# Nine attention blocks ahead of the MLP, x through DRAM, and the weight decode on VectorE

## The chip, the core and the metric

One core of a Trainium2 chip runs the whole program in one launch. TensorE (PE) multiplies, VectorE (DVE) and ScalarE (ACT) do the elementwise work, GpSimd (POOL) some of it and the scattered stores, and SyncE (SP) issues most transfers. The metric is the device time of one execution in microseconds, the median of three runs.

## The reference

```python
def _attn_ref(u, v, z):
    scores = scale * np.matmul(z, z.transpose(0, 2, 1))   # 8 x 3072 x 3072, d_qk 64
    attn = np.maximum(scores, 0.0) ** 2
    out = np.matmul(attn, v)                              # d_model 256
    return (u * out).astype(np.float32)

def _moe_ref(x, w_in, w_out):                             # 24576 tokens, 256 -> 2048 -> 256
    h = x @ w_in
    g = h * (1.0 / (1.0 + np.exp(-h)))
    return (g @ w_out).astype(np.float32)

def _moe2_ref(x, w_gate, w_output_gate, w1, w2):          # 8 experts, 256 -> 1024 -> 256
    e_idx = np.argmax(x @ w_gate, axis=1)
...
        h = np.maximum(x[mask] @ w1[e], 0.0)
        out[mask] = gate_w[mask, None] * eom[mask, e, None] * (h @ w2[e])
```

The output of the first feeds the second, and that of the second the third. The scores are symmetric, since the same z stands on both sides.

## The kernel before

The attention's work is 48 blocks of 512 queries (n = 6 b + q, six for each of eight batches b), and a block has 24 steps, one for each tile of 128 keys. Every factor is kept as a high and a low part in float32r, and each product is three matmuls (high by high, low by high, high by low).

- A **direct step** has 2 matmuls of 512 columns for the scores (L269, L270), Relu and Square on ACT (L272, L273), the high part on ACT (L275) or DVE (L277), the low part on DVE (L251), and 6 matmuls of 512 columns into the accumulator `acc` (L293 to L295).
- A **mirrored step** takes the scores of an earlier block of the same batch instead of computing them. The earlier block stored them in the DRAM tile `sym` (L239). SP loads them with four transfers for each step (L225), DVE transposes (L232) and makes the low part, ACT the high part, and 6 matmuls follow. A block q has 4 q mirrored steps, from block 3 on. The loads go through `raw`, which has four buffers, together with the loads of z and V.
- An **MLP step** is one sixteenth of the MLP of a block's 512 tokens: 6 matmuls of 512 columns (L324), a sigmoid on ACT (L326), a product on DVE (L328), the high part on ACT (L331), the low part on DVE (L333), and 12 matmuls of 256 columns into `acc` (L358 to L360). After the last step ACT copies `acc` into the record `rec` with two copies (L350). PSUM has two buffers for `acc`: where attention and MLP alternate, each has one.

After its MLP a block is routed: 32 dot products of `rec` with the gate's weights on DVE (L368, the program calls them dots), some small operations that pick the expert, a count on PE (L375), and four scattered stores on POOL (L434) into the DRAM tile `scr`. When 46 blocks are routed, a snapshot of the counts (L456 to L483) sets up the first 39 tiles of 512 tokens of the third part, which SP loads from `scr` (L572). 22 smaller tiles come behind. This third part is the same in both kernels.

The sixteen 512-column pieces of the MLP's weights are decoded on chip (`w_decode`, `w_parts`): each is loaded into a `rec` buffer (L825), and takes seven operations on DVE (L840 to L843, L854 to L856), one on ACT and two on POOL (L857, L858). Of batch 0 POOL also makes the low parts of V (L94).

One list of steps sets the order on all engines. A step's front part is issued at its place, the middle one place later and its products three places later (`LOOK`). Other work (loads, decode, dots, stores) is a list of tasks, each with a due place, a release place and a cost. A step gives a budget, which pays for tasks that are released but not yet due, in the order of their due places, and the search stops after 60 entries that are not released:

```python
                if rel <= i and budget <= 0:
                    break
                k += 1
                if k > 60:
                    break
```

Before, blocks 0 and 1 and the first seven steps of block 2 run alone, then the MLP of block 0 alone, then that of block 1 step by step with block 2. From block 3 on two MLP steps stand ahead of every three attention steps. The loads of u and the product with the attention's output (`finish`, L303) go into the buffer `xf`, and the split of x (L204, L206) follows at once, so x never leaves the chip.

## Time and profile before

| | |
|---|---|
| median of three runs | 5292.82 us (5292.71 to 5293.24) |
| profiled execution, its own time | 5293.77 us |
| its span in the profile | 5292.0 us |
| PE busy | 5189.7 us, 98% |
| DVE, ACT, POOL busy | 3897.6, 3234.9, 491.2 us |

A PE matmul's record is longer than its share of the engine, since they are pipelined: PE's pace is read from one start to the next. What PE loses is the length of a stretch less the matmuls in it at that pace.

### The profile page before, as it was taken

How to read it: one execution, taken by the hardware profiler on the slowest of the kernel's cores; microseconds unless marked ns; L12 is line 12 of the kernel's file. 1: busy time of each engine (PE TensorE's matmuls, PEld its weight loads, DVE VectorE, ACT ScalarE, POOL GpSimd, SP SyncE). 2: the span in 40 equal slices, each digit the busy share in tenths (PEclk: the TensorE clock that was granted, in tenths of full speed). 3: DMA queues.
4: the chain of work that ended last, by engine and by line, in shares of the span. 5: the costliest groups of instructions: out<-in, count | busy, mean ns of one | idle time of the engine just before them, and what ended most of it. 6: DMA issues, size and time to landing. Idle time of an engine off the chain costs nothing.

```text
span 5292.0 us, 88328 instructions
## 1 busy us (share of the span) xinstructions
PE 5189.7 (98%) x30026; PEld 4529.6 (86%) x30026; DVE 3897.6 (74%) x9627; ACT 3234.9 (61%) x5804; POOL 491.2 (9%) x503
## 2 busy tenths in 40 slices
PE   7999999999999999999999999999999899999998
PEld 5888888888888888888888888888888799999998
DVE  8778767866786778677767877687677786666687
ACT  6655665666566666665666566656654455555576
POOL 3100000000000000000000000000000121111111
PEclk9999999999999999999999999999999899999999
DMA  5134324433442334234333432343333456555564
GB/s 155 57 81 86 102 80 92 93 89 77 86 104 85 81 77 110 81 77 84 108 80 82 87 106 75 83 91 95 86 83 80 133 171 201 175 175 175 178 229 157
DMA packets 1334523, 574.63 MB, mean 109 GB/s; under 512 B 1173421, under 2 KB 1206830, under 8 KB 1318192
## 3 DMA queue, kind: packets, MB, share of 16 engines
q1 hardware_dynamic: 1315248, 517.00, 38.1%
q0 software_dynamic: 18816, 51.93, 2.7%
q8 instruction: 237, 3.88, 0.3%
q14 instruction: 222, 1.82, 0.1%
HBM read 393.54 MB, written 178.42 MB: 108 GB/s over the span
## 4 chain that ended last, share of the span: by engine, by line
PE 84%; DVE 8%; ACT 3%; issue 2%; DMA 2%; SPq 0%; POOL 0%; DVEq 0%; ACTq 0%; POOLq 0%
PE ps L324 17%; PE ps L663 10%; PE acc L360 9%; PE acc L358 9%; PE acc L359 9%; PE acc L295 8%; PE acc L294 8%; PE acc L293 8%; PE ps L269 3%; PE ps L270 3%; DVE lo L251 1%; DMA raw<-sym 1%; DVE lo L333 1%; DVE junk L368 1%; DVE t L328 1%
## 5 line engine op out<-in xcount | busy, mean ns | idle before, releaser
L328 DVE TENSOR_TENSOR t<-ps,t 128x512 f32<-128x512 f32 x768 | 529.4, 689 | 655.5 <-ACT t L326 649.8
L359 PE MATMUL acc<-woutl,hi 128*128 128x256 f32 x3600 | 998.3, 277 | 0.0
L331 ACT ACTIVATE hi<-t 128x512 fp32r<-128x512 f32 x768 | 486.0, 633 | 764.1 <-DVE t L328 764.1
L294 PE MATMUL acc<-lo,vh 128*128 128x512 f32 x2304 | 911.1, 395 | 37.7 <-DVE lo L251 37.5
L295 PE MATMUL acc<-hi,vl 128*128 128x512 f32 x2304 | 910.9, 395 | 0.0
L293 PE MATMUL acc<-hi,vh 128*128 128x512 f32 x2304 | 903.3, 392 | 0.0
L360 PE MATMUL acc<-wouth,lo 128*128 128x256 f32 x3072 | 858.5, 279 | 42.5 <-DVE lo L333 42.4
L251 DVE TENSOR_TENSOR lo<-t,hi 128x512 fp32r<-128x512 f32 x1152 | 791.4, 688 | 130.9 <-ACT hi L275 128.9
L358 PE MATMUL acc<-wouth,hi 128*128 128x256 f32 x3072 | 853.9, 278 | 0.0
L359 PEld LDWEIGHTS acc<-woutl,hi 128*128 128x128 f32 x3600 | 678.0, 188 | 32.4
L368 DVE CUSTOM_DVE_ANT_0 junk<-rec,wg 128x256 f32<-128x256 f32 x1536 | 648.7, 422 | 35.3
L360 PEld LDWEIGHTS acc<-wouth,lo 128*128 128x128 f32 x3072 | 577.9, 188 | 53.0 <-DVE lo L333 50.9
L326 ACT ACTIVATE t<-ps 128x512 f32<-128x512 f32 x768 | 454.6, 592 | 265.5 <-PE ps L324 263.7
L358 PEld LDWEIGHTS acc<-wouth,hi 128*128 128x128 f32 x3072 | 577.6, 188 | 26.2
L294 PEld LDWEIGHTS acc<-lo,vh 128*128 128x128 f32 x2304 | 433.9, 188 | 158.3 <-DVE lo L251 56.5
L434 POOL DMA_INDIRECT scr<-rec,si x192 | 206.7, 1077 | 3767.2 <-DVE lo L251 1705.9
L264 ACT ACTIVATE hi<-t 128x512 fp32r<-128x512 f32 x468 | 295.8, 632 | 418.7 <-DVE t L232 333.9
L333 DVE TENSOR_TENSOR lo<-t,hi 128x512 fp32r<-128x512 f32 x768 | 523.6, 682 | 13.1 <-issue 0.2
L293 PEld LDWEIGHTS acc<-hi,vh 128*128 128x128 f32 x2304 | 434.2, 188 | 98.8
L295 PEld LDWEIGHTS acc<-hi,vl 128*128 128x128 f32 x2304 | 434.3, 189 | 91.4
L666 ACT ACTIVATE hi<-ps 128x512 fp32r<-128x512 f32 (+1 forms) x488 | 254.7, 522 | 396.9 <-PE ps L663 375.3
L668 DVE SCALAR_TENSOR_TENSOR lo<-ps,hi 128x512 fp32r<-128x512 f32 (+1 forms) x488 | 288.2, 591 | 245.8 <-ACT hi L666 244.0
(449 smaller groups left out, 10572.9 us busy)
## 6 DMA issues: line engine op xcount, KB each, us to landing
raw<-in_w_dram SPq DMA_DIRECT2D x122, 1024.0 KB
sym<-t SPq DMA_DIRECT2D x468, 256.0 KB
raw<-sym SPq DMA_DIRECT2D x1872, 64.0 KB
raw<-in_zT_dram SPq DMA_DIRECT2D x192, 128.0 KB
raw<-in_vp_dram SPq DMA_DIRECT2D x96, 256.0 KB
xf<-in_uT_dram SPq DMA_DIRECT2D x96, 256.0 KB
xg<-scr SPq DMA_DIRECT2D x39, 544.0 KB
x<-scr SPq DMA_DIRECT2D x304, 64.0 KB
```

The lines of the kernel that those rows point to most:

```text
L251: nc.vector.tensor_tensor(out=lo, in0=a, in1=r32(hi), op=ALU.subtract)
L293: nc.tensor.matmul(acc[:, c, :], h, hi, start=i == 0, stop=False)
L294: nc.tensor.matmul(acc[:, c, :], h, lo, start=False, stop=False)
L295: nc.tensor.matmul(acc[:, c, :], l, hi, start=False, stop=i == KT - 1)
L324: nc.tensor.matmul(ps, win_at(w, c, f_), x[c], start=c == 0 and i == 0, stop=c == ND - 1 and i == 2)
L328: nc.vector.tensor_tensor(out=g, in0=ps, in1=sg, op=ALU.mult)
L333: return lambda: nc.vector.tensor_tensor(out=lo, in0=g, in1=r32(hi), op=ALU.subtract)
L358: nc.tensor.matmul(y[:, s, :], a, wh, start=first and s % per_bank == 0, stop=False, skip_group_check=True)
L359: nc.tensor.matmul(y[:, s, :], a, wl, start=False, stop=False, skip_group_check=True)
L360: nc.tensor.matmul(y[:, s, :], l, wh, start=False, stop=last, skip_group_check=True)
L368: nc.vector.tensor_tensor_reduce(out=j, in0=a, in1=w, scale=1.0, scalar=0.0, op0=ALU.mult, op1=ALU.add, accum_out=res)
L663: nc.tensor.matmul(ps[:, 0:T], w[:, o:o + P], y[c][:, 0:T], start=c == 0 and j == 0, stop=c == ND - 1 and j == 2)
```

## The change

Blocks 0 to 8 run their attention alone, ahead of any MLP step. Their x therefore has to wait, and goes to DRAM: `finish` stores each half (two transfers for each block), and `load_x` brings it back through `raw` shortly before the MLP block, where `f_x` splits it. From block 9 on, an attention block takes 24, 22, 20, 18, 16 or 14 MLP steps by its place q in the batch, in eight groups, each ahead of three attention steps. An MLP block of 16 steps no longer ends where an attention block does.

The mirrored steps begin at block 4 of batch 0, so block 3's twelve become direct. POOL's part of the decode goes to DVE (`w_low`), and so do the low parts of V of batch 0. The decode tasks are released from place 24. The dots of block 45 become due ten places ahead of the last MLP block, where they were due at the end of the one before it.

```diff
@@ the constants
-EARLY = 0.95
+EARLY = 0.75
+LEAD = 9
+MIX = (24, 22, 20, 18, 16, 14)
...
-PRE = 7
@@ x of a block, kept in DRAM until its MLP block
         def load_u(b, q):
             t = mk(cp, [P, ND, TQ], F32, "xf", 1)
...
+        def load_x(n, c):
+            def f(t):
+                nc.sync.dma_start(out=t, in_=xd[n][:, c, :])
+            return f
+
+        def f_x(n, c):
+            def f(t):
+                if c == 0:
...
+                h, l = xs[n]
+                nc.scalar.activation(h[c], t, AF.Copy)
+                nc.vector.tensor_tensor(out=l[c], in0=t, in1=r32(h[c]), op=ALU.subtract)
+            return f
...
         def mirrored(b, q, k):
-            return k // NS < q and (b, q) >= (0, 3)
+            return k // NS < q and (b, q) >= (0, 4)
@@ att_items
-            early = (b, q) < (0, 2)
+            early = b * NQ + q < LEAD
...
-                    if (early and q and k % 2) or (not early and (q or k % 3)):
+                    if k % 2 and b + q or not early and (q or k % 3):
                         nc.scalar.activation(hi, a, AF.Copy)
                     else:
                         nc.vector.tensor_copy(hi, a)
...
                     if i == KT - 1:
                         later(1, 1.2, finish, 0)
-                        later(3, 1.2, lambda: split_x(b, q, hold == "last"), 0)
...
             def finish():
-                for c, x in enumerate(xs[(b, q)]):
+                n = b * NQ + q
+                xd[n] = dram.tile([P, ND, TQ], F32, name=f"x_{n}")
+                for c in range(ND):
+                    x = st["x"][:, c, :]
                     nc.vector.scalar_tensor_tensor(out=x, in0=st["acc"][:, c, :], scalar=AS, in1=x, op0=ALU.mult, op1=ALU.mult)
+                    nc.sync.dma_start(out=xd[n][:, c, :], in_=x)
@@ the order of the steps
-        order = [("a", 0, 0, KT), ("a", 1, 0, KT), ("a", 2, 0, PRE), ("m", 0, 0, NF1)]
-        for k in range(NF1):
-            order += [("a", 2, PRE + k, PRE + k + 1), ("m", 1, k, k + 1)]
...
-        for n in range(3, NBLK):
+        order = [("a", n, 0, KT) for n in range(LEAD)]
+        GA, todo = KT // 8, 0
+        for n in range(LEAD, NBLK):
             for g in range(8):
-                if n > 3 or g >= 2:
-                    j = (g - 2) % 8 * GM
-                    owed.append(("m", n - 1 if g >= 2 else n - 2, j, j + GM))
...
+                for _ in range(MIX[n % NQ] * (g + 1) // 8 - MIX[n % NQ] * g // 8):
+                    m = todo // NF1
+                    if (m + 1, 4) <= (n, g):
+                        order += [("m", m, todo % NF1, todo % NF1 + 1)]
+                        todo += 1
                 order += [("a", n, g * GA, (g + 1) * GA)]
...
+        for todo in range(todo, NBLK * NF1):
+            order += [("m", todo // NF1, todo % NF1, todo % NF1 + 1)]
@@ V, the loads of x, the decode and the route
-            return lambda t: split(t, hi, lo, due, None if b else nc.gpsimd)
+        def f_split(hi, lo, due):
+            return lambda t: split(t, hi, lo, due)
...
+            for c in range(ND):
+                prep(moe_at[n] - 3 + c, moe_at[n] - 3 + c if n == NBLK - 1 else moe_end[n - 2] if n > 1 else moe_at[0] - 4, load_x(n, c), f_x(n, c), att_step(n, KT - 1) + LOOK + 4)
...
-                nc.gpsimd.tensor_tensor(out=m, in0=t_bits, in1=r32(hi), op=ALU.subtract)
-                nc.gpsimd.tensor_tensor(out=lo, in0=m, in1=t_rem, op=ALU.add)
...
+        def w_low(k):
...
+                nc.vector.tensor_tensor(out=m, in0=t_val[k % 2], in1=r32(hi), op=ALU.subtract)
+                nc.vector.tensor_tensor(out=lo, in0=m, in1=t_rem, op=ALU.add)
                 w_load(k + 2)
...
-            task(job[0], 6, 1.9, w_decode(k))
-            task(job[0], 6, 1.3, w_parts(k))
+            task(job[0], KT, 2.4, w_decode(k))
+            task(job[0], KT, 1.6, w_parts(k))
+            task(job[0], KT, 1.4, w_low(k))
...
+            if n == NBLK - 3:
+                due = moe_at[NBLK - 1] - 10
             route_tasks(n, due, rel)
```

Three places show the order.

On PE, at the end of an MLP block in the middle of the kernel before (`acc_18534` is the MLP's accumulator, `acc_19339` the attention's, `ps` the scores or the MLP's first product):

```order
L358 MATMUL acc_18534<-wouth_99,hi_19357 128x256
L359 MATMUL acc_18534<-woutl_101,hi_19357 128x256
L360 MATMUL acc_18534<-wouth_99,lo_19358 128x256
L324 MATMUL ps_19434<-xo_19317,winh_94 128x512
L324 MATMUL ps_19434<-xo_19317,winl_96 128x512
L324 MATMUL ps_19434<-x_19318,winh_94 128x512
L324 MATMUL ps_19434<-xo_19317,winh_94 128x512
L324 MATMUL ps_19434<-xo_19317,winl_96 128x512
L324 MATMUL ps_19434<-x_19318,winh_94 128x512
L293 MATMUL acc_19339<-hi_19367,vh_115 128x512
```

The next MLP block's own products begin 24 matmuls further on. In the change, at the first such end (`acc_4314` and `acc_5157` are two MLP blocks' accumulators):

```order
L367 MATMUL acc_4314<-wouth_99,hi_5066 128x256
L368 MATMUL acc_4314<-woutl_101,hi_5066 128x256
L369 MATMUL acc_4314<-wouth_99,lo_5067 128x256
L275 MATMUL ps_5148<-hh_4015,hl_107 128x512
L276 MATMUL ps_5148<-ll_4016,hl_107 128x512
L367 MATMUL acc_5157<-wouth_98,hi_5089 128x256
L368 MATMUL acc_5157<-woutl_100,hi_5089 128x256
L369 MATMUL acc_5157<-wouth_98,lo_5090 128x256
```

Two matmuls of a direct step stand between an MLP block's last product and the next MLP block's first, and the attention's products come behind. On ACT the copies of that accumulator stand between two direct steps:

```order
L279 ACTIVATE t_1162_5125<-t_1162_5125 128x512
L281 ACTIVATE hi_5120<-t_1162_5125 128x512
L359 ACTIVATE rec_5142<-acc_4314 128x2x256 x2
L278 ACTIVATE t_1167_5151<-ps_5148 128x512
L279 ACTIVATE t_1167_5151<-t_1167_5151 128x512
```

There are 22 such ends in the change, and none before: 14 with a direct front between, as here, and 8 with nothing, where the front is that of a mirrored step.

On SP, in block 5 before (`sym_2_5` holds scores for mirrored steps, `zT` is z):

```order
L162 DMA raw_4810<-in_zT_dram 64x512
L163 DMA raw_4810<-in_zT_dram 64x512
L225 DMA raw_4881<-sym_2_5_2529 32x16x32 x4
L225 DMA raw_4898<-sym_2_5_2529 32x16x32 x4
L225 DMA raw_4925<-sym_2_5_2529 32x16x32 x4
L225 DMA raw_4948<-sym_2_5_2529 32x16x32 x4
L225 DMA raw_5001<-sym_3_5_3398 32x16x32 x4
L225 DMA raw_5018<-sym_3_5_3398 32x16x32 x4
L225 DMA raw_5045<-sym_3_5_3398 32x16x32 x4
```

and in the change, where between these loads no MLP step runs and a weight piece is loaded (`rec`, L833):

```order
L163 DMA raw_2476<-in_zT_dram 64x512
L164 DMA raw_2476<-in_zT_dram 64x512
L231 DMA raw_2495<-sym_2_5_1410 32x16x32 x4
L231 DMA raw_2512<-sym_2_5_1410 32x16x32 x4
L833 DMA rec_2529<-in_win_dram 128x1024
L231 DMA raw_2533<-sym_2_5_1410 32x16x32 x4
L231 DMA raw_2551<-sym_2_5_1410 32x16x32 x4
L231 DMA raw_2558<-sym_3_5_1822 32x16x32 x4
L231 DMA raw_2579<-sym_3_5_1822 32x16x32 x4
```

The weights' loads stood at rows 13 to 78 of SP before, and 14 of the 16 now stand among the tiles of blocks 4 to 9.

On DVE, the dots of block 45 before, ahead of the snapshot (L328 and L333 belong to MLP steps, `L` are the results):

```order
L333 TENSOR_TENSOR lo_46448<-t_10847_46445,hi_46447 128x512
L368 ISA junk_46486,L_45918<-rec_45831,wg 128x256
L368 ISA L_45918 128x1
L368 ISA junk_46488,L_45918<-rec_45831,wg 128x256
L368 ISA L_45918 128x1
L328 TENSOR_TENSOR t_10859_46499<-ps_46490,t_10858_46497 128x512
L333 TENSOR_TENSOR lo_46471<-t_10852_46468,hi_46470 128x512
L368 ISA junk_46517,L_45918<-rec_45831,wg 128x256
L368 ISA L_45918 128x1
L368 ISA junk_46519,L_45918<-rec_45831,wg 128x256
L368 ISA L_45918 128x1
L368 ISA junk_46521,L_45918<-rec_45831,wg 128x256
```

and in the change (L337 and L342 are the MLP's; the lines left out are more of L377):

```order
L337 TENSOR_TENSOR t_10884_46531<-ps_46522,t_10883_46529 128x512
L342 TENSOR_TENSOR lo_46484<-t_10874_46481,hi_46483 128x512
L337 TENSOR_TENSOR t_10889_46558<-ps_46549,t_10888_46556 128x512
L342 TENSOR_TENSOR lo_46534<-t_10884_46531,hi_46533 128x512
L377 ISA junk_46577,L_46576<-rec_46468,wg 128x256
L377 ISA L_46576 128x1
L377 ISA junk_46579,L_46576<-rec_46468,wg 128x256
L377 ISA L_46576 128x1
...
L377 ISA junk_46639,L_46576<-rec_46468,wg 128x256
L377 ISA L_46576 128x1
L410 TENSOR_REDUCE m_46641<-L_46576 128x4
```

All 32 dots of the block now follow on one another, before the pick (L410), whose result PE's count needs (`L384 MATMUL ps_46658<-ohc,ones 128x8`), and this count stands ahead of the next MLP front on PE.

## Rows read from the trace of the kernel before

**Rows 1.** The page's part 1, busy time by engine.

```profile
PE 5189.7 (98%) x30026; PEld 4529.6 (86%) x30026; DVE 3897.6 (74%) x9627; ACT 3234.9 (61%) x5804; POOL 491.2 (9%) x503
```

**Rows 2.** Windows by attention block (0, 1, 2, 6): length, busy, counts, clock.

```profile
core 0: us, PE busy (x) PEld busy (x) DVE busy (x) ACT busy (x) POOL busy (x), PEclk, DMA share, GB/s
6.80:74.20 67.40, 52.87 (x198) 38.34 (x199) 59.04 (x86) 46.92 (x82) 28.78 (x21) 0.97 0.56 174
74.20:137.90 63.70, 50.58 (x193) 37.25 (x192) 61.31 (x91) 46.81 (x80) 22.42 (x16) 0.95 0.46 132
137.90:277.10 139.20, 135.64 (x772) 117.22 (x771) 100.34 (x208) 88.34 (x152) 20.30 (x17) 1.00 0.18 58
520.50:612.80 92.30, 90.27 (x487) 76.47 (x486) 66.58 (x177) 65.56 (x114) 9.27 (x10) 1.00 0.35 112
```

**Rows 3.** Timeline of PE: start, duration, line, tile; 512 columns, then 256.

```profile
400.11 0.40 PE L295 MATMUL acc<-hi,vl 128*128 128x512 f32 x1
400.34 0.40 PE L324 MATMUL ps<-xo,winh 128*128 128x512 f32 x1
...
4090.29 0.28 PE L359 MATMUL acc<-woutl,hi 128*128 128x256 f32 x1
4090.41 0.28 PE L360 MATMUL acc<-wouth,lo 128*128 128x256 f32 x1
```

**Rows 4.** Waits of PE in the first 150 us: total, times, longest.

```profile
PE acc L294 <- DVE lo L251: 28.8, 25, 2.5
```

**Rows 5.** Timeline of DVE and of POOL in block 0.

```profile
55.07 1.77 DVE L251 TENSOR_TENSOR lo<-t,hi 128x512 fp32r<-128x512 f32 x1
...
58.69 0.67 DVE L251 TENSOR_TENSOR lo<-t,hi 128x512 fp32r<-128x512 f32 x1
59.29 0.41 DVE L840 TENSOR_SCALAR wg<-wg 128x512 f32<-128x512 f32 x1
...
54.96 1.33 POOL L857 TENSOR_TENSOR wg<-junk,wouth 128x512 f32<-128x512 f32 x1 [5.61 <-DVE wg L856]
56.37 1.63 POOL L858 TENSOR_TENSOR woutl<-wg 128x512 fp32r<-128x512 f32 x1
```

**Rows 6.** Waits of SP's queue in the first 150 us.

```profile
SPq L825 <- DVE wg L855: 81.4, 13, 10.9
```

**Rows 7.** Timeline of SP (three mirrored tiles) and of DVE (one mirrored step).

```profile
4030.14 6.14 SPq L225 DMA_DIRECT2D raw<-sym  x12
...
4055.42 0.70 DVE L232 STREAM_TRANSPOSE t<-raw 128x512 f32<-128x512 f32 x1
...
4056.62 0.70 DVE L232 STREAM_TRANSPOSE t<-raw 128x512 f32<-128x512 f32 x1
```

**Rows 8.** Timeline of PE and ACT at an MLP block's end.

```profile
877.16 0.28 PE L360 MATMUL acc<-wouth,lo 128*128 128x256 f32 x1
...
878.67 0.40 PE L293 MATMUL acc<-hi,vh 128*128 128x512 f32 x1
...
877.53 1.09 ACT L350 ACTIVATE rec<-acc 128x512 f32<-128x512 f32 x2
```

**Rows 9.** Timeline of PE, POOL and ACT around 4100 us.

```profile
4122.62 0.58 PE L360 MATMUL acc<-wouth,lo 128*128 128x256 f32 x1 [23.78 <-DVE lo L333]
4123.00 0.41 PE L358 MATMUL acc<-wouth,hi 128*128 128x256 f32 x1
4123.21 0.41 PE L359 MATMUL acc<-woutl,hi 128*128 128x256 f32 x1
...
4108.45 0.99 POOL L434 DMA_INDIRECT scr<-rec,si  x1 [96.47 <-DMA xg<-scr]
...
4119.67 1.09 ACT L350 ACTIVATE rec<-acc 128x512 f32<-128x512 f32 x2 [26.18 <-DMA scr<-rec,si]
```

**Rows 10.** Timeline of DVE: two dots of the route.

```profile
399.82 0.41 DVE L368 CUSTOM_DVE_ANT_0 junk<-rec,wg 128x256 f32<-128x256 f32 x1
...
400.28 0.42 DVE L368 CUSTOM_DVE_ANT_0 junk<-rec,wg 128x256 f32<-128x256 f32 x1
```

More of the change, by code (lines that the diff above doesn't have):

```diff
@@ L63, in moe_chain @@
     NBM = min(NB, (N - NA * TQ) // TB + E // 2)
-    assert NBLK > 3 and KT >= PRE + NF1 and KT % 8 == 0 and NF1 % 8 == 0 and NF1 >= 16 and NA <= P and NB <= P and N // P <= 256
+    assert NBLK > 3 and KT % 8 == 0 and NF1 >= 16 and NA <= P and NB <= P and N // P <= 256
     ZS = 2.0 ** -10
@@ L182, in moe_chain @@
         xs = {}
+        xd = {}
         def load_u(b, q):
             t = mk(cp, [P, ND, TQ], F32, "xf", 1)
[L187 removed]
             for c in range(ND):
[L189 to L206 removed]
+                nc.sync.dma_start(out=t[:, c, :], in_=uT[b, q, :, c, :])
+            return t
+        def load_x(n, c):
[5 more added lines that the diff above has]
+                if c == 0:
+                    if n == NBLK - 1:
+                        r = mk(cp, [P, NS, RW], F32, "rec", 2).rearrange("p s c -> p (s c)").bitcast(F32R)
+                        h = r[:, 0:ND * TQ].rearrange("p (c t) -> p c t", t=TQ)
+                        l = mk(cp, [P, ND, TQ], F32R, "x", 1)
+                    else:
+                        h, l = (mk(ap_ if g == "xo" else cp, [P, ND, TQ], F32R, g, 1) for g in (("xo", "x") if n % 2 else ("xh", "xl")))
+                    xs[n] = [h[:, i, :] for i in range(ND)], [l[:, i, :] for i in range(ND)]
+                h, l = xs[n]
+                nc.scalar.activation(h[c], t, AF.Copy)
+                nc.vector.tensor_tensor(out=l[c], in0=t, in1=r32(h[c]), op=ALU.subtract)
+            return f
         def mirrored(b, q, k):
[L210 removed]
+            return k // NS < q and (b, q) >= (0, 4)
         def key_order(b, q):
@@ L239, in keep, with att_items @@
             nc.sync.dma_start(out=sym[key][k % NS * P:(k % NS + 1) * P, :], in_=a)
-        def att_items(b, q, hold):
+        def att_items(b, q):
             st = {}
-            early = (b, q) < (0, 2)
+            early = b * NQ + q < LEAD
             ks = key_order(b, q)
@@ L318, in f @@
                 def f():
-                    xh, xl = xs[(b, q)]
+                    xh, xl = xs[n]
                     ps = psum()
@@ L701, in moe_chain @@
         blocks = [(b, q) for b in range(B) for q in range(NQ)]
-        order = [("a", 0, 0, KT), ("a", 1, 0, KT), ("a", 2, 0, PRE), ("m", 0, 0, NF1)]
-        for k in range(NF1):
-            order += [("a", 2, PRE + k, PRE + k + 1), ("m", 1, k, k + 1)]
-        order += [("a", 2, PRE + NF1, KT)]
-        GA, GM = KT // 8, NF1 // 8
-        owed = []
-        for n in range(3, NBLK):
-            for g in range(8):
-                if n > 3 or g >= 2:
-                    j = (g - 2) % 8 * GM
-                    owed.append(("m", n - 1 if g >= 2 else n - 2, j, j + GM))
-                if n < NBLK - 1 or g < 6:
-                    order += owed
-                    owed = []
+        assert NQ == len(MIX) and LEAD < NBLK
+        order = [("a", n, 0, KT) for n in range(LEAD)]
+        GA, todo = KT // 8, 0
+        for n in range(LEAD, NBLK):
+            for g in range(8):
+                for _ in range(MIX[n % NQ] * (g + 1) // 8 - MIX[n % NQ] * g // 8):
[3 more added lines that the diff above has]
+                        todo += 1
                 order += [("a", n, g * GA, (g + 1) * GA)]
-        order += owed + [("m", NBLK - 2, 6 * GM, NF1), ("m", NBLK - 1, 0, NF1)]
+        for todo in range(todo, NBLK * NF1):
+            order += [("m", todo // NF1, todo % NF1, todo % NF1 + 1)]
         steps = {}
         for n, bq in enumerate(blocks):
-            steps["a", n] = att_items(*bq, "last" if n == NBLK - 1 else None)
+            steps["a", n] = att_items(*bq)
             steps["m", n] = moe_items(*bq)
@@ L742, in prep @@
         def prep(due, rel, load, use, since=0):
-            stream.append((due, rel, len(stream), load, use, since))
+            stream.append((due, max(rel, since), len(stream), load, use, since))
         def used(n, keys):
@@ L856, in f @@
                 v.scalar_tensor_tensor(out=t_rem, in0=t_rem.bitcast(I32), scalar=2.0 ** -44, in1=m, op0=ALU.mult, op1=ALU.mult)
-                nc.gpsimd.tensor_tensor(out=m, in0=t_bits, in1=r32(hi), op=ALU.subtract)
-                nc.gpsimd.tensor_tensor(out=lo, in0=m, in1=t_rem, op=ALU.add)
+            return f
+        def w_low(k):
+            def f():
+                hi, lo = wjobs[k][2:]
+                m = wbig[k]
+                nc.vector.tensor_tensor(out=m, in0=t_val[k % 2], in1=r32(hi), op=ALU.subtract)
+                nc.vector.tensor_tensor(out=lo, in0=m, in1=t_rem, op=ALU.add)
                 w_load(k + 2)
```

23 lines of the change are left out of this document (2 added, 21 removed).

## The prediction, made before the change was run

> **What bounds the kernel now.** First the busy times [rows 1]: PE has records for 98% of the span, DVE for 74%, ACT for 61%. So the question at each place is what PE loses. A PE record is longer than PE's pace, which is read from start to start: 0.23 us for 512 columns and 0.12 for 256 [rows 3]; over long fed stretches I take 0.229 and 0.1145. Times the counts of the windows this gives the loss of a stretch. Block 0: 67.4 less 198 x 0.229 = 45.3 is 22.1, and with the 6.8 before the first matmul 28.9. Block 1: 63.7 less 193 x 0.229 = 44.2 is 19.5. Block 2 has 32 MLP steps, so 384 of its 772 matmuls have 256 columns: 388 x 0.229 + 384 x 0.1145 = 132.8 of 139.2, a loss of 6.4. Block 6 with 16 MLP steps: 295 x 0.229 + 192 x 0.1145 = 89.5 of 92.3, a loss of 2.8 [rows 2]. I put blocks 2 to 8 at 18 together, and so blocks 0 to 8 at 67. Next the waits: in the first 150 us PE waits 28.8 us in 25 pieces for DVE's low parts [rows 4], and the timelines say why: one low part took 1.77 us while POOL ran an operation of the decode, and 0.67 when it did not [rows 5]. The last place is at 4100 us, where PE stands still for 23.78 us: an MLP low part waits in a chain behind ACT's copy into `rec`, that copy behind a scattered store, and the store behind the first loads of the third part [rows 9]. Behind it PE runs at 0.21 for 256 columns, half its pace, for a few us, so the whole costs about 26. From block 9 on little is lost: a round of six blocks like that of block 6 loses some 8 us, about 51 over blocks 9 to 46.
>
> **Attention alone in blocks 0 to 8.** A direct step is 8 x 0.229 = 1.83 us of PE, a mirrored one 6 x 0.229 = 1.37. Block 3's twelve mirrored steps become direct, which is 24 matmuls, **+5.5 us** of PE. MLP steps that leave these blocks come back later, unchanged. Without POOL the stretched low parts go. Of block 0's 28.9 the start stays (6.8 and the first step's chain, together about 10), and ACT has 47.5 us of operations there against 45.3 of PE, so I leave 15. Blocks 1 to 3 have 20 of DVE and 38 of ACT beside 44 of PE, since the decode does not reach them: its tasks stand behind more than 60 unreleased mirrored loads, and the search ends there. I give them 1.7 in all. The decode then falls on blocks 4 to 9. A job is three DVE operations of two inputs at 0.60 (start to start of the low part that was not stretched [rows 5]) and four of one input at some 0.43, 3.5 us, and gets two more at 0.60: 4.7; sixteen are 75 us. Block 5 has 20 mirrored steps in a row. SP issues three tiles in 6.14 us [rows 7], so 2.05 for each against PE's 1.37; DVE takes 1.20 for each [rows 7], and 3.5 jobs in that stretch add 16.5, so 20 x 1.20 + 16.5 = 40.5 against 20 x 1.37 = 27. SP's 20 x 2.05 are 41 as well, so the loss is 14; with the order of the queue, where a weight's load stands among the tiles' loads and waits for DVE, I take 17 (14 to 26). Block 4 has 16 of them, 12 after the four tiles that are loaded ahead: 12 x 2.05 and the loads of z and u, some 32 us against 20.6: 11 (6 to 16). Block 6 gets V and decode jobs, 4; blocks 7 and 8 5; block 9 1.5. The sum is 15 + 1.7 + 11 + 17 + 4 + 5 + 1.5 = 55 (45 to 66) against 67: **-12** (-22 to -1). If the cover were whole it would be -50.
>
> **The end of MLP blocks.** Before, the attention block's products and another front lie between two MLP blocks, and the copies are hidden: the last product starts at 877.16 and lasts 0.28, the two copies run from 877.53 to 878.62, and the next products, of the other accumulator, start at 878.67 [rows 8]. The next MLP block needs the copied buffer 24 matmuls further on. In the change 22 ends have another MLP block's products right behind. Those write the buffer that the copies read, so they can't start before 878.62 on this scale, 1.35 after PE would be free (877.16 + 0.1145). With a direct front between, 2 x 0.229 = 0.46 of that is covered: 14 x 0.89 + 8 x 1.35 = 23. Where ACT is in the middle of another operation the wait grows by up to its length: 32. I take **+26** (20 to 32). Nobody waits in turn: DVE and ACT have their next step's inputs and use the pause.
>
> **The route of block 45 and the tail.** The stores of block 45 now come before the loads of the third part, so the 23.78 us wait goes. What is late next is the snapshot. It needs all 32 dots of block 45, which now stand in a row on DVE: 32 x 0.467 (two dots are 0.46 apart [rows 10]) = 15, and 2.6 of small operations behind, and PE's count for it stands ahead of the next MLP front. So PE waits some 18, and 2 for the half pace behind it, 20 of the 26: **-6** (-15, if DVE starts the row while PE still has work, to +2).
>
> **Steady blocks 9 to 46.** Each block adds two stores and two loads of 256 KB to SP, some 1.8 us of issue by the u loads beside the tiles, on a queue that has two thirds of a block free. The split of x costs what it did. A block with many mirrored tiles gets 14 or 16 MLP steps as cover, that with the loads of V 24. I leave these 51 us at **0** change (-13 to +13): the ends are a fourth of what is lost there.
>
> **The sum.** 5.5 - 12 + 26 - 6 + 0 = +13.5 on the profiled execution's 5293.8, that is 5307.3. The profiled execution is 1.0 above the median of the three runs, so the median is **5306**.
>
> **Rivals.** *Faster: the mix pays.* In a round the losses lie at the block that loads V and at the one whose tiles and z loads share SP. If 24 MLP steps beside the first and 16 beside the second cover them, the 51 of the steady blocks fall to 20: 5306 - 31 = **5275**. For it: the loss comes from bursts (block 6 loses 2.8 of 92.3 with DVE busy only 72% of it [rows 2]), which a longer block dilutes. Against: the same number of dots, loads and splits remains. *Slower: the decode's loads hold SP.* SP's queue waited 81.4 us in 13 pieces for DVE before a weight could be loaded, up to 10.9 in one [rows 6]; that cost nothing while nothing urgent stood behind. Now tiles do. If three such waits of 10.9 fall in blocks 4 and 5, that is 33 more: **5339**. It decides where DVE is over a tile's time behind SP; against it, SP is itself late there, so DVE has mostly passed. *Slower still: the clock.* In block 1, with 19 us of short waits, the granted clock was 0.95, in block 6 with 2.8 it was 1.00 [rows 2]. If each of the 22 new pauses dropped the clock as the long wait did, at the 2 us that I put for it, that would be 44: **5350**. The Trainium skill (TensorE: Matmul & The Clock Gate, A second HAM failure mode: psum-queue depth-cycling) says of a kernel that cycled through PSUM banks that PE's small pauses between groups were enough to make the clock swing between its levels. The trace does not bear it out so far: with 25 pauses of up to 2.5 in 150 us [rows 4] the clock stayed at 0.95 and 0.97 of its full level [rows 2]. *The change doesn't do what it says:* the decode is not spread over nine blocks but falls into four to nine; that is in the forecast already, and if it did spread, blocks 4 and 5 would lose 12 less: 5294, no change.
>
> **How the numbers follow.** This kernel's measurement can tell some 0.2%, or 10.6 us, from no change: faster is under 5282.2, slower over 5303.4. Forecast 0.52, in itself 5288 to 5324 (slower 0.26, same 0.22, faster 0.04); the mix 0.25 (faster 0.20, same 0.05); the queue 0.12 and the clock 0.05, slower; the spread decode 0.06 (same 0.05, faster 0.01). So slower 0.43, same 0.32, faster 0.25. Eight in ten lie from 5270 to 5330.
>
> **What would show it.** In the profile after: no row of POOL beside a low part of blocks 0 to 3, and a loss of under 2 in each of 1 to 3; SP solid through blocks 4 and 5, and PE waiting for `lo` (L257 there, behind the transpose) some 28 in both; 22 waits of an MLP block's first product for ACT's `rec` copy (L359), of 0.9 to 1.5 each; at block 47 one wait of about 18 at the count (L384) in place of 23.78. I am wrong if the first products show no waits (then 26 less), or if blocks 4 and 5 run at PE's pace, or if a block such as 12 or 16 gains or loses more than 2.

## The result and the profile after

The change made the kernel slower: the median went from 5292.8 to 5353.4 us (four runs from 5347.7 to 5359.3), a ratio of 1.0113, with a 95% interval of 1.0101 to 1.0126. The forecast was slower too, but at 5306, with a range that ended at 5330. The profiled execution took 5359.25, the longest of the four, with a span of 5357.0 against 5292.0 before. So 65 us are to be found between the two profiles, 4 more than between the medians.

The page's first part, and the waits of PE over the whole run of the change (what waited and for whom, total us, times, longest):

```profile
PE 5216.8 (97%) x30050; PEld 4540.6 (85%) x30050; DVE 3888.8 (73%) x9687; ACT 3236.6 (60%) x5800; POOL 414.0 (8%) x459
...
PE acc L300 <- DVE lo L257: 55.1, 57, 3.8
PE acc L367 <- ACT rec L359: 34.4, 22, 2.7
PE ps L384 <- DVE ohc L423: 17.7, 1, 17.7
PE acc L369 <- DVE lo L342: 10.6, 28, 1.2
```

The second and third rows are new. The 22 waits of an MLP block's first product (L367) for ACT's copy (L359) are the ends of MLP blocks that the prediction counted, and the single one of 17.7 is the count behind block 45's dots; the 23.78 of [rows 9] is gone.

Where the 65 us lie is seen from PE's starts. The table gives what PE lost between the last products of attention blocks: of each distance from one matmul's start to the next, what it has above 0.230 (512 columns) or 0.115 (256), summed with its sign, so that shorter distances count against longer ones. The first matmul itself (6.8 before, 6.2 after) comes on top.

| PE's loss, us | blocks 0 to 8 | blocks 9 to 46 | block 47 and the third part |
|---|---|---|---|
| before | 58.6 | 40.5 | 39.0 |
| the change | 70.7 | 90.9 | 36.4 |
| ends mended (e1_gap) | 73.3 | 50.3 | 31.9 |
| batch 0 all direct (e3_direct0) | 28.9 | 83.6 | 33.2 |
| x through DRAM alone (e7_xonly) | 60.1 | 51.9 | 39.1 |
| four blocks ahead (e5_lead4) | 35.9 | 58.8 | 24.3 |
| the same, more decode early (e11_lead4e) | 28.5 | 48.9 | 26.7 |

With the 5.5 us of added matmuls and the first matmul's 0.6: 12.1 - 0.6 + 50.4 - 2.6 + 5.5 = 64.8, which is the 65 of the spans. These are single executions: the six runs below that keep the change's order from block 9 on lost 83 to 91 in the middle column, so that some 7 of the 50.4 can belong to this execution.

**Blocks 3 to 6.** Windows of the change (length, busy time and count of each engine, granted clock, DMA share and GB/s), to be held against [rows 2]:

```profile
core 0: us, PE busy (x) PEld busy (x) DVE busy (x) ACT busy (x) POOL busy (x), PEclk, DMA share, GB/s
149.50:193.90 44.40, 44.40 (x194) 36.09 (x193) 21.34 (x39) 36.77 (x62) 0.00 (x0) 1.00 0.26 89
193.90:248.20 54.30, 42.68 (x161) 31.13 (x160) 39.42 (x67) 26.41 (x45) 0.00 (x0) 0.94 0.70 141
248.20:303.70 55.50, 41.55 (x153) 29.03 (x152) 44.65 (x77) 22.90 (x39) 0.00 (x0) 0.94 0.77 157
303.70:361.20 57.50, 48.18 (x193) 36.31 (x192) 39.10 (x72) 44.84 (x79) 0.00 (x0) 0.97 0.66 197
```

Block 3 (first row) loses 0.2, as blocks 1 and 2 do: DVE has little to do (21 us), and there is no decode, as the count of 39 operations says. Blocks 4 and 5 lose 17.6 and 20.6, block 6 13.4. DVE isn't full in them (39 and 45 of 55), but its queue stands still often. These are its four largest waits from 193.9 to 303.7:

```profile
DVE t L238 <- DMA raw<-sym: 10.7, 14, 1.4
DVE hi L283 <- ACT t L279: 6.2, 5, 2.1
DVE hl L169 <- ACT hl L168: 5.8, 5, 2.5
DVE ll L175 <- ACT hh L174: 3.2, 2, 2.5
```

DVE's work (84.1) and these waits (25.9) fill the 109.8 us of the two blocks. PE's matmuls there are 71.4 (36 mirrored steps of 1.37 and 12 direct ones of 1.83). So what the two blocks lose is 12.7 of DVE's work beyond PE's, 10.7 of waits for tiles and 15.2 of waits for ACT, 38.6 in all.

The longest wait of PE there, on SP, ACT, DVE and PE (an idle time before an operation stands in brackets):

```profile
225.63 0.47 SPq L163 DMA_DIRECT2D raw<-in_zT_dram  x1
...
229.82 0.63 ACT L168 ACTIVATE hl<-raw 128x512 fp32r<-128x512 f32 x1 [1.72 <-DMA raw<-in_zT_dram]
230.49 0.69 DVE L169 TENSOR_TENSOR hl<-raw,hl 64x512 fp32r<-64x512 f32 x1 [2.55 <-ACT hl L168]
233.94 0.50 PE L300 MATMUL acc<-lo,vh 128*128 128x512 f32 x1 [3.82 <-DVE lo L257]
235.27 0.63 PE L301 MATMUL acc<-hi,vl 128*128 128x512 f32 x1
235.70 0.63 PE L275 MATMUL ps<-hh,hl 128*128 128x512 f32 x1
```

A load of z was issued at 225.63 among the tiles, ACT waited for it, and DVE, which takes its operations in order, waited for ACT with the next tile behind it. When PE went on, it ran at 0.43 for 512 columns, half its pace, for a few us: the granted clock of blocks 4 and 5 is 0.94, and by PE's starts some 7 of their 38 us were lost at this pace. In block 6 the longest piece begins on ACT, which waited for a stored tile to leave its buffer, and PE then waited twice, 4.4 of the 13.4:

```profile
343.12 0.60 ACT L278 ACTIVATE t<-ps 128x512 f32<-128x512 f32 x1 [6.17 <-DMA sym<-t]
...
345.10 0.49 PE L299 MATMUL acc<-hi,vh 128*128 128x512 f32 x1 [2.16 <-ACT hi L281]
347.82 0.80 PE L300 MATMUL acc<-lo,vh 128*128 128x512 f32 x1 [2.23 <-DVE lo L257]
```

**An end of an MLP block**, at 1330 us, on ACT and PE, to be held against [rows 8]:

```profile
1329.55 0.62 ACT L210 ACTIVATE xh<-raw 128x512 fp32r<-128x512 f32 x1
1330.07 0.57 ACT L278 ACTIVATE t<-ps 128x512 f32<-128x512 f32 x1
1330.67 0.63 ACT L279 ACTIVATE t<-t 128x512 f32<-128x512 f32 x1
1331.34 0.63 ACT L281 ACTIVATE hi<-t 128x512 fp32r<-128x512 f32 x1
1331.88 1.07 ACT L359 ACTIVATE rec<-acc 128x512 f32<-128x512 f32 x2
...
1329.92 0.28 PE L369 MATMUL acc<-wouth,lo 128*128 128x256 f32 x1
...
1332.99 0.39 PE L367 MATMUL acc<-wouth,hi 128*128 128x256 f32 x1 [2.33 <-ACT rec L359]
...
1334.08 0.41 PE L368 MATMUL acc<-woutl,hi 128*128 128x256 f32 x1
1334.30 0.41 PE L369 MATMUL acc<-wouth,lo 128*128 128x256 f32 x1
```

The last product of the old block is at 1329.92. Before, the copies began 0.37 after it. Here ACT first finishes a split of x and a whole direct step (Relu, Square, copy) that stand ahead in its order, so they begin at 1331.88, and PE's first product of the new block waits for the second copy. From 0.9 us behind this wait PE runs at 0.21 for 256 columns, for some 3 us. That is not so behind every long wait. Here the pace stays whole:

```profile
1645.93 0.39 PE L367 MATMUL acc<-wouth,hi 128*128 128x256 f32 x1 [2.45 <-ACT rec L359]
1646.15 0.28 PE L368 MATMUL acc<-woutl,hi 128*128 128x256 f32 x1
1646.27 0.28 PE L369 MATMUL acc<-wouth,lo 128*128 128x256 f32 x1
```

### The profile page after: what moved, and what is told of

Its sections match the earlier page's. It is cut to its first block, busy times and chain, and to the rows that moved or that the text cites. A ratio compares the mean times of both kernels' runs of the same rounds, so it can differ in the third digit from the quotient of the medians.

```text
span 5357.0 us, 88803 instructions
## 1 busy us (share of the span) xinstructions
PE 5216.8 (97%) x30050; PEld 4540.6 (85%) x30050; DVE 3888.8 (73%) x9687; ACT 3236.6 (60%) x5800; POOL 414.0 (8%) x459
## 4 chain that ended last, share of the span: by engine, by line
PE 82%; DVE 7%; ACT 4%; DMA 3%; issue 3%; SPq 1%; DVEq 0%; ACTq 0%; POOLq 0%; POOL 0%
PE ps L333 17%; PE ps L672 10%; PE acc L367 9%; PE acc L369 9%; PE acc L368 9%; PE acc L300 8%; PE acc L301 8%; PE acc L299 7%; PE ps L275 3%; PE ps L276 3%; DMA raw<-sym 1%; DVE junk L377 1%; DVE t L238 1%; DVE lo L257 1%; DVE t L337 1%
## 5 line engine op out<-in xcount | busy, mean ns | idle before, releaser
L337 DVE TENSOR_TENSOR t<-ps,t 128x512 f32<-128x512 f32 x768 | 530.1, 690 | 702.9 <-ACT t L335 686.4
L300 PE MATMUL acc<-lo,vh 128*128 128x512 f32 x2304 | 915.4, 397 | 55.3 <-DVE lo L257 55.1
L367 PE MATMUL acc<-wouth,hi 128*128 128x256 f32 x3072 | 858.9, 280 | 34.4 <-ACT rec L359 34.4
L369 PE MATMUL acc<-wouth,lo 128*128 128x256 f32 x3072 | 859.1, 280 | 11.0 <-DVE lo L342 10.6
L257 DVE TENSOR_TENSOR lo<-t,hi 128x512 fp32r<-128x512 f32 x1152 | 772.9, 675 | 105.2 <-ACT hi L281 99.2
L377 DVE CUSTOM_DVE_ANT_0 junk<-rec,wg 128x256 f32<-128x256 f32 x1536 | 648.9, 422 | 34.5
L367 PEld LDWEIGHTS acc<-wouth,hi 128*128 128x128 f32 x3072 | 578.8, 188 | 67.5 <-ACT rec L359 42.0
L342 DVE TENSOR_TENSOR lo<-t,hi 128x512 fp32r<-128x512 f32 x768 | 520.8, 678 | 7.7
```

The source lines that it names most:

```text
L257: nc.vector.tensor_tensor(out=lo, in0=a, in1=r32(hi), op=ALU.subtract)
L300: nc.tensor.matmul(acc[:, c, :], h, lo, start=False, stop=False)
L337: nc.vector.tensor_tensor(out=g, in0=ps, in1=sg, op=ALU.mult)
L342: return lambda: nc.vector.tensor_tensor(out=lo, in0=g, in1=r32(hi), op=ALU.subtract)
L367: nc.tensor.matmul(y[:, s, :], a, wh, start=first and s % per_bank == 0, stop=False, skip_group_check=True)
L369: nc.tensor.matmul(y[:, s, :], l, wh, start=False, stop=last, skip_group_check=True)
```

## The experiments

### The ends of MLP blocks

```diff
+GAP = 2
...
+        flat = [(kind, n, k) for kind, n, k0, k1 in order for k in range(k0, k1)]
+        i = 0
+        while i + 1 < len(flat):
+            if flat[i][0] == flat[i + 1][0] == "m" and flat[i + 1][2] == 0:
+                nxt = [j for j in range(i + 2, len(flat)) if flat[j][0] == "a"][:GAP]
+                for s_, j in enumerate(nxt):
+                    flat.insert(i + 1 + s_, flat.pop(j))
+            i += 1
+        order = [(kind, n, k, k + 1) for kind, n, k in flat]
```

> Only the order of steps changes: wherever an MLP block's last step is followed by the next MLP block's first, two attention steps are put between. Theory A (the ends of MLP blocks cost what the profile after shows there: 34.4 us of waits for ACT's copies in 22 places, and some 6 more of slow restarts): the waits go and the median falls from 5353 by about 40, to 5313 (5306 to 5322). Rival B (the pauses only show lateness of ACT and DVE that must be paid anyway): the waits move to the low parts, and the time stays within 8 us of 5353.

It took 5316.5 (5315.0 to 5318.5), 37 less than the change. The waits of PE in that run:

```profile
PE acc L301 <- DVE lo L258: 55.1, 55, 4.0
PE ps L385 <- DVE ohc L424: 18.0, 1, 18.0
PE acc L370 <- DVE lo L343: 13.1, 31, 1.7
```

No wait for ACT's copies is left, and the waits for the low parts are nearly as they were (55.1 both times, 13.1 for 10.6), so the pauses did not move there. Theory A holds. In blocks 9 to 46 the loss went from 90.9 to 50.3, so the ends cost some 40 by the profiles and 37 by the medians. 21 of the 22 waits lie there, with 33.1 us; behind four of these PE lost about 6 more at half pace, and the rest was not taken apart.

### The decode and the search for tasks

```diff
-                if k > 60:
+                if k > (600 if i < LEAD * KT else 60):
```

> The search for released tasks goes 600 entries deep while blocks 0 to 8 run, instead of 60, so the decode can fall into blocks 1 to 3, where DVE is busy for 46% of PE's time. Theory A (the decode in blocks 4 to 8 lengthens DVE's part there): the losses of blocks 4 to 8, 61.5 us together in the profile after, fall by some 20, to 5333 (5325 to 5343). Rival B (these blocks wait for tiles and z loads alone): within 5 us of 5353.

It took 5347.9 (5345.7 to 5352.6), 5.5 less, at the edge of rival B. The windows of blocks 1, 4 and 5 (columns as above) say why it was no clean test:

```profile
61.90:106.20 44.30, 44.30 (x193) 36.04 (x192) 37.25 (x70) 39.88 (x68) 0.00 (x0) 1.00 0.40 119
...
196.30:256.10 59.80, 42.97 (x161) 31.00 (x160) 47.63 (x83) 28.27 (x48) 0.00 (x0) 0.94 0.72 145
256.10:310.30 54.20, 40.45 (x154) 29.11 (x154) 43.54 (x75) 23.23 (x39) 0.12 (x1) 0.94 0.70 141
```

Block 1 took decode work at no loss (DVE 37 us where it had about 21, loss 0.2). But the budget of 0.75 a step paid for only ten of the 16 jobs in blocks 1 to 3, and the other six came in blocks 4 and 5. In the change these have four, blocks 6 to 8 nine and block 9 three. With two jobs more, blocks 4 and 5 lost 42 together for 38. Block 6 (13.4 to 8.5) and block 8 (6.1 to 2.4) fell. So the decode's nine jobs cost up to 10 us in blocks 6 to 8, and what blocks 4 and 5 lose without any decode no run with their mirrored steps alone shows.

### The mirrored steps of batch 0

```diff
-            return k // NS < q and (b, q) >= (0, 4)
+            return k // NS < q and (b, q) >= (1, 0)
...
-                        due = att_step(n - 2, KT // 2 + 2 * j) if j < NQ - 2 else ...
+                        due = att_step(n, j * NS) - 3 if n == NQ else att_step(n - 2, KT // 2 + 2 * j) if j < NQ - 2 else ...
```

> No mirrored steps in batch 0: the 36 of blocks 4 and 5 are computed, which is 72 more matmuls of 512 columns, 16.5 us. The loads of z for batch 1 move into block 6. Theory A (the mirrored tiles without MLP steps beside them cost blocks 4 and 5 their 38 us): these losses fall to some 4, a net gain of 17, to 5336 (5328 to 5345). Rival B (the losses come from decode and z loads whatever the steps are): the 16.5 us are added, about 5370.

It took 5323.8 (5322.6 to 5328.0), 30 less although PE has 16.5 more to do, and more than theory A's 17. Blocks 4 and 5 lose 1.2 and 4.1, with four decode jobs in them as in the change. Their windows:

```profile
195.50:240.80 45.30, 44.60 (x194) 35.98 (x193) 37.14 (x70) 39.95 (x68) 0.00 (x0) 1.00 0.21 64
240.80:289.00 48.20, 45.97 (x193) 35.42 (x192) 36.87 (x66) 43.78 (x77) 0.13 (x1) 1.00 0.35 109
```

In block 4 DVE's busy time is nearly that of the change (37 against 39; in block 5 it is 37 against 45), so its load alone isn't what that block lost to: with the tiles went the DMA share (0.70 to 0.21), and the clock is whole. Theory A holds in kind: without MLP steps beside them, mirrored steps cost more than the matmuls that they save. The gain beyond theory A lies in blocks 6 to 8, which lose 11.7 for 22.5: with no mirrored loads ahead of it in the list the search found the decode earlier, ten of its jobs ran in blocks 1 to 3, and two were left for these blocks.

### What of a mirrored step it is

Only the loads of z were moved in the first of three runs:

```diff
-                        due = att_step(n - 2, KT // 2 + 2 * j) if j < NQ - 2 else ...
+                        due = att_step(n, j * NS) - 3 if n == NQ else att_step(n - 2, KT // 2 + 2 * j) if j < NQ - 2 else ...
```

> Only the loads of z for batch 1 move: from blocks 4 and 5, where they stand between the mirrored tiles, into block 6. Theory A (DVE's and ACT's queues stand still behind a z load that lands 3 us after its issue, and that is much of blocks 4 and 5): their losses fall from 38 to about 23, block 6 gains 5 of loss: 5343 (5337 to 5348). Rival B (SP's issue of tiles is the limit, and z's 10 us of issue are only moved): blocks 4 and 5 fall by no more than the 10 that leave, block 6 rises by as much: within 5 us of 5353.

It took 5360.7 (5360.2 to 5361.1), 7 more. Blocks 4 and 5 lost 34.8 for 38.2, and blocks 6 to 8 lost 29.4 for 22.5. Theory A falls, and the time is 2 us beyond what rival B allowed: the standstill behind a z load is what the longest wait looks like, but the time is only paid elsewhere when the load goes.

The other two change the tile's load alone. Four transfers of plain rows:

```diff
-                    nc.sync.dma_start(out=t[g * SQ:(g + 1) * SQ].rearrange("t (j d) -> t j d", d=SQ),
-                                      in_=src[:, o:o + SQ].rearrange("(j t) d -> t j d", t=SQ))
+                    nc.sync.dma_start(out=t[g * SQ:(g + 1) * SQ], in_=src[o:o + SQ, :])
```

> The change, but a mirrored tile's four loads take plain rows of 2 KB of the stored scores instead of 32 by 32 pieces, so that a tile is 128 packets and not 2048; the scores then stand in the wrong order (the output isn't the reference's). SP issues as many transfers as in the change. Theory A (SP's issue of four transfers a tile, 2.05 us, is what blocks 4 and 5 wait for): their losses stay at 33 to 40 together, the time within 6 us of 5353. Theory B (the 16 DMA engines' time for 2048 small packets is): they fall under 15, the time to 5325 or less.

and one transfer:

```diff
-                for g in range(P // SQ):
...
+                o = k % NS * P
+                nc.sync.dma_start(out=t, in_=src[o:o + P, :])
```

> As the run before, but one transfer a tile instead of four: 128 packets and a fourth of the issues (the scores stand in the wrong order, so the output isn't the reference's). Theory A (SP's issue): the losses of blocks 4 and 5 fall from 38 to some 10, and the time to 5325. Theory B (packets): the same as with four transfers of rows, within 3 us. If neither falls, the cause is DVE's and ACT's own queue in these blocks.

They took 5342.6 and 5331.8. The losses of blocks 4 and 5 together were 38.2 in the change, 31.2 with rows in four transfers and 23.2 with one. DVE's waits in the two blocks, first with four transfers, then with one:

```profile
DVE hl L169 <- ACT hl L168: 7.1, 5, 3.1
DVE hi L282 <- ACT t L278: 6.2, 5, 2.1
DVE t L237 <- DMA raw<-sym: 2.8, 5, 0.8
```

```profile
DVE hi L281 <- ACT t L277: 6.2, 5, 2.1
DVE hl L169 <- ACT hl L168: 3.6, 5, 0.7
DVE ll L175 <- ACT hh L174: 1.5, 2, 0.7
```

The 10.7 us of waits for tiles shrink to 2.8 and then vanish. So neither theory is the whole of it: plain rows save 7, one transfer in place of four saves 8 more, and 23 stay when tiles come at once. The first step is not the packets alone, since SP also issues rows faster. Twelve transfers in a row, in the change and then with rows in four transfers:

```profile
200.27 6.29 SPq L231 DMA_DIRECT2D raw<-sym  x12
200.59 5.49 SPq L231 DMA_DIRECT2D raw<-sym  x12
```

The windows of blocks 4 and 5 with one transfer:

```profile
193.20:238.60 45.40, 41.32 (x162) 31.39 (x161) 38.97 (x67) 26.20 (x45) 0.00 (x0) 0.92 0.54 168
238.60:288.10 49.50, 40.51 (x153) 30.09 (x152) 44.61 (x77) 23.35 (x40) 0.00 (x0) 0.93 0.57 176
```

The 23 that stay are DVE's: of the 94.9 us it works 83.6, 12 more than PE's 71.4, and its waits for ACT, the three rows above, are the other 11.3. The Trainium skill (DMA: Bandwidth & Descriptors, Why small descriptors are slow (HBM only)) says that every small descriptor carries a fixed overhead. The trace agrees: the DMA engines were busy for 0.70 and 0.77 of the two blocks with 2048 packets of 128 bytes to a tile, and for 0.54 and 0.57 with 128 of 2 KB, at more GB/s.

### POOL

```diff
-            return lambda t: split(t, hi, lo, due)
+            return lambda t: split(t, hi, lo, due, None if b else nc.gpsimd)
...
-                nc.vector.tensor_tensor(out=m, in0=t_val[k % 2], in1=r32(hi), op=ALU.subtract)
-                nc.vector.tensor_tensor(out=lo, in0=m, in1=t_rem, op=ALU.add)
+                nc.gpsimd.tensor_tensor(out=m, in0=t_val[k % 2], in1=r32(hi), op=ALU.subtract)
+                nc.gpsimd.tensor_tensor(out=lo, in0=m, in1=t_rem, op=ALU.add)
```

> The two operations of each decode job, and the low parts of V of batch 0, go back to POOL; all else is as in the change. Theory A (POOL beside DVE stretches DVE's operations by about 1 us each, 32 operations of the decode and 12 of V, and the blocks it falls on have no slack on DVE): 20 us slower, 5373 (5362 to 5385). Rival B (what counts is that DVE has 1.2 us less to do for each job): 10 to 15 us faster, 5340.

It took 5360.9 (5355.5 to 5363.6), 7.5 more. The loss of blocks 0 to 8 rose from 70.7 to 77.4. Neither number was right. The runs of the two kernels overlap (the change reached 5359.3), so the 7 us are hardly clear of the spread. They lie in the direction of theory A and are a third of its size.

### x through DRAM by itself

The order of steps of the kernel before stands here, with each MLP block one group later, so that x has time to come back, and everything else but x's way is as before. The edit of the order, against the kernel before:

```diff
-                if n > 3 or g >= 2:
-                    j = (g - 2) % 8 * GM
-                    owed.append(("m", n - 1 if g >= 2 else n - 2, j, j + GM))
+                if n > 3 or g >= 3:
+                    j = (g - 3) % 8 * GM
+                    owed.append(("m", n - 1 if g >= 3 else n - 2, j, j + GM))
```

> Of the change only x's way through DRAM is kept: the order of steps, the mirrored steps, the decode with POOL and the due place of block 45's dots are those of the kernel before, but each MLP block begins one group (three attention and two MLP steps) later. Theory A (x through DRAM costs nothing where SP has time): 5293, within 6 us. Rival B (the four transfers for each block and the splits at other places make the steady blocks 9 to 46 slower by the 10 us that are left there when the ends are mended): 5303 (5300 to 5310).

It took 5307.7 (5306.3 to 5312.0), a ratio of 1.0027 (1.0018 to 1.0037). In blocks 9 to 46 the loss is 51.9 for 40.5: theory B, where the prediction had put zero. Of the 11, 4.4 are in the six blocks that load V (12, 18 and so on), 3.6 in the six ahead of them, and the rest in the others. In the kernel before, block 18 had three waits of up to 0.9; now it has one of 2 us, on ACT, DVE and PE:

```profile
1566.15 1.06 ACT L359 ACTIVATE rec<-acc 128x512 f32<-128x512 f32 x2
1567.10 0.60 ACT L335 ACTIVATE t<-ps 128x512 f32<-128x512 f32 x1
...
1567.73 0.69 DVE L337 TENSOR_TENSOR t<-ps,t 128x512 f32<-128x512 f32 x1 [3.62 <-ACT t L335]
...
1569.07 0.50 PE L300 MATMUL acc<-lo,vh 128*128 128x512 f32 x1 [2.05 <-DVE lo L257]
```

ACT has V's high parts and the record's copies in a row, DVE stands 3.62 us for ACT's sigmoid, and the attention's low part stands behind. Part of this may come from the MLP block's start, which is one group later than before; the run doesn't part the two. The steady blocks of the run with mended ends lose the same 50 in sum, but at other places: the six V blocks 14 (24 in the kernel before, 28 here), the seven with z loads beside their tiles (10, 16 and so on) 15 (14 and 16), all others 21 (2 and 7). So the equal sums don't show that the change pays the same price.

### Four blocks ahead

```diff
-LEAD = 9
+LEAD = 4
...
-                if k > 60:
+                if k > (600 if i < LEAD * KT else 60):
```

with the two attention steps between MLP blocks.

> Only four attention blocks, all direct, run ahead (the mix starts at block 4), with the deeper search for the decode and with two attention steps put between MLP blocks. Theory A (in blocks 4 to 8 it is the tiles' loads and stores that have no MLP steps beside them): the losses of blocks 0 to 8 fall from 70.7 to some 25, and the ends' 37 go too: 5271 (5262 to 5282), faster than the kernel before. Rival B (the loads cost the same with MLP steps beside them, or the decode, now on three blocks, takes it back): 5295 or more.

It took 5279.4 (5275.9 to 5280.7), a ratio of 0.9971 (0.996 to 0.9982) to the kernel before. Blocks 5 to 8, with MLP steps beside their tiles, lose 1.5, 1.4, 0.3 and 1.4. Only block 4 lost, 20.0, and there not to tiles: six decode jobs came due at once, and DVE had 57 us of work in the 63 us to 260. Raising the budget of a step in the blocks ahead mends that:

```diff
-EARLY = 0.75
+EARLY = 1.15
```

> Four blocks ahead, the deeper search and two attention steps between MLP blocks, as in the run that reached 5279, and a step's budget for other work in the blocks ahead raised from 0.75 to 1.15, so that nearly the whole decode falls into blocks 1 to 3 (DVE has 24 x 1.0 us free in each, a job takes 4.7). Theory: block 4's loss of 20.0 there came from the last six jobs, of 4.7 each, that came due at once; it falls to some 5, at a price of up to 5 in blocks 1 to 3: 5268 (5262 to 5275). Rival (blocks 1 to 3 lose what block 4 gains): 5279, within 4 us.

It took 5263.5 (5261.8 to 5267.4), a ratio of 0.9942 (0.9925 to 0.9958): faster than both kernels. The windows of blocks 1 and 4:

```profile
66.90:113.70 46.80, 45.75 (x193) 35.58 (x192) 44.58 (x85) 41.89 (x72) 0.00 (x0) 1.00 0.41 136
...
209.30:289.40 80.10, 80.10 (x446) 69.44 (x445) 55.03 (x89) 50.13 (x86) 0.00 (x0) 1.00 0.53 116
```

Block 4 has 16 mirrored steps and loses 0.1 of 80. The price is a loss of 2.7 in each of blocks 1 to 3, where DVE is now nearly as busy as PE, and 6 more in block 0. Against the kernel before, the table gives 30 less in blocks 0 to 8, 12 less behind them and 8 more in between. Without the two steps between MLP blocks (which is the only edit):

> The run of four blocks ahead with the budget of 1.15 (5263), but without the two attention steps between MLP blocks: in nine places one block's last step is followed by the next one's first again. Theory (each end costs 1.3 to 2.8 us and its slow restart): 9 x 1.7 = 15 more, 5279 (5273 to 5283). Rival (the gain of that run came from the places of steps around, not from the ends): within 4 us of 5263.

it took 5273.4 (5273.1 to 5276.5), 10 more than with them. The theory holds with a smaller size: the waits for the copies came in seven places and not nine, 9.3 us in all.

Last, nine blocks ahead with what was found mended:

```diff
-EARLY = 0.75
+EARLY = 1.15
...
-            return k // NS < q and (b, q) >= (0, 4)
+            return k // NS < q and (b, q) >= (1, 0)
```

with the deeper search, the later loads of z and the steps between MLP blocks.

> Nine blocks still run ahead, but what cost time there and at the ends is mended at once: no mirrored steps in batch 0 (16.5 us more of PE), two attention steps between MLP blocks, the deeper search and a budget of 1.15. Theory (the faults add up): 5353 less 37, less 30, less 6, 5280 (5272 to 5289), faster than the kernel before. Rival (with the mirrored steps gone the decode and the loads of batch 1 come to stand in each other's way in block 6): 5290 or more.

It took 5302.2 (5299.8 to 5304.0), a ratio of 1.0015 (1.0005 to 1.0024). The gains didn't add up: blocks 0 to 8 lose 44.2, where the run with direct steps alone lost 28.9. The rival named the wrong place, though. 16.7 of the 44 are in block 0 and 2.7 to 2.9 in each of blocks 1 to 3, 13 more than with the budget of 0.75. That is the price of the same budget that saved 20 in block 4 of the run above; here no block had six jobs to do at once. Blocks 5 and 6 lose 15.6 (13.0 with direct steps alone) although no decode is left in them, so the rival's two causes are not needed together: the loads of batch 1 are there without the decode, and whether they alone cost this was not tested.

## Why the prediction was wrong

The sign was right, to which the prediction itself gave 0.43, and most mechanisms were at their places. But three terms of the sum were too small, all in one direction: the lead by 23.5 us, the ends by 14, the steady blocks by 10, which is 48 of the 51.5 between 13.5 and 65.

1. **Blocks 0 to 3**: right. Block 0 lost 9.4 and the first 6.2, 15.6 where 15 stood; blocks 1 to 3 lost 0.6 where 1.7 stood, with no decode in them, as the order had told.
2. **Blocks 4 to 8**: mis-sized. Blocks 4 and 5 lost 38 where 28 stood (their range went to 42), and blocks 6 to 8 22.5 where 9 stood. In blocks 4 and 5 the step that failed is that the larger of SP's 41 and DVE's 40.5 was taken as the time of the stretch. DVE's load was read well (44.7 in block 5, with its four direct steps), but its waits came on top of it: 10.7 for tiles, in which SP's lateness shows, and 15.2 for ACT, to which the sum gave nothing. The runs on the tile's load bear this out: when the tiles came at once, the 10.7 were gone, the waits for ACT fell to 11.3, and 23 of the 38 stayed. The clock, 0.94 in both blocks, which the sum left out, has some 7 of the 38. Blocks 6 to 8 are the larger part of the miss, 13.5, and had been given 4 and 5 without a working. The run with the deeper search puts up to 10 of it to the decode's nine jobs there; in block 6 the wait for stored tiles was not in the prediction at all. The lead's term was -12; by the table, the blocks' loss with the first matmul is 76.9 for 65.4, +11.5.
3. **The rival on SP's queue** (the weights' loads hold up the tiles) has no support: in block 5 SP waited 0.4 us for a weight's buffer, where 10.9 had been feared. SP did stand 8.7 us for DVE there, ahead of the store of x at 250.22 and with block 5's tiles behind it. But `raw` was full by then, and the next tile went out at 253.37, when DVE's transpose had freed a buffer.
4. **The ends of MLP blocks**: the mechanism and the count of 22 were right, and the size was 40 by the profiles, 37 by the medians, for 26. The prediction took ACT as free when the last product ends, as in [rows 8], and allowed for the rest of one operation. The row at 1330 shows three or four operations ahead of the copies; the mean wait is 34.4 / 22 = 1.56, on top of the 0.46 that is covered where a direct front stands between.
5. **The clock rival** was partly true. Of the 22 waits six were of 1.96 to 2.66 us, and behind four of them (such as 2.33 at 1333) PE ran at half pace for some 3 us; behind 2.45 at 1645.93, 1.96 and all that were shorter it didn't. The prediction called 25 pauses of up to 2.5 that left 0.95 no evidence for it; they were some. That the rival's time, 5350, is near the result is chance, since its 44 us aren't there: four times 1.6 are.
6. **Steady blocks**: 0 stood, about +10 came, by the run with mended ends (50.3 for 40.5). The range of -13 to +13 held it. The step that failed is that nothing was given to the new order and to x's way. The run with x through DRAM alone loses 11 more as well, but at other places, so the cause in the change stays open. *The mix pays* was half right: with the ends mended, the V blocks beside 24 MLP steps lose 14 for 24, as it said, in the blocks with z loads nothing is gained (15 for 14), and the other blocks, which lost 2, lose 21.
7. **The tail**: right in its mechanism, 17.7 for 18 at the count. The third column fell by 2.6, where -6 stood; one of the 22 ends lies in it.

By terms, the profiles' 65 are 5.5 + 11.5 + 50.4 - 2.6. The range was built from single terms' spreads as if they could cancel, and in the first two they had a cause in common: where the change puts work of one kind next to its like (tiles beside tiles, ends beside ends), an in-order queue gets it in a row, and each term was priced by the work and not by what stands ahead of it in the queue. For the steady blocks this is not shown.

What stays open: what blocks 4 and 5 would lose without decode, how the 7 us that plain rows save divide between packets and SP's issue, where the steady blocks' 10 us come from, and whether the 11 us of x through DRAM by itself come from its transfers or from the places of its splits.

## What to carry to other kernels

Running ahead paid here as long as what ran ahead was bound by PE alone: direct blocks took three decode jobs each at a loss of 0.2 and five at 2.7, and the fifth block's transposed loads needed MLP steps beside them again. Where two blocks of work share a double-buffered accumulator with a third, don't let one's end touch the next one's beginning; price such a place by everything that stands in the copying engine's queue ahead of the copy, not by the copy. When two in-order engines are both near the bound of a stretch, take one engine's work plus its waits for the other as the pessimistic end, and not the larger of the two as the middle.

## What the runs showed of the hardware

A single pause of 2.3 us in an otherwise full stretch was followed by some 3 us at the lower clock level (0.21 for 256 columns), which cost about 1.6 more. Its length alone did not decide: one of 2.45 us at 1645.93 was followed by none, and neither was the same end's pause, 2.32 us at 1305.6, in the run with batch 0 all direct. SP took 0.52 us to issue a transfer of 32 by 32 pieces and 0.46 for one of the same 64 KB in plain rows. POOL's share in the decode mattered little: some 7 us, hardly clear of the spread, for 32 operations of 1.3 to 1.6 us and the low parts of V, although beside them one low part on DVE took 1.77 us and not 0.67 [rows 5].
